# Second batch masked on VectorE, mask table built on chip, smaller value loads between the w_out pieces

## The chip, the core and the metric

The kernel runs on one core of one Trainium2 chip. The metric is the device time of one execution in microseconds; three executions of the kernel before gave 304.31, 306.18 and 306.58 us, so 306.18 us is its median. The profile is of one execution, which also took 306.18 us.

A core has engines with an instruction queue each, which works strictly in order: PE (TensorE, matmuls; PEld is its loading of weights), DVE (VectorE), ACT (ScalarE), POOL (GpSimd) and SP (SyncE, which here only starts DMA transfers). They wait for one another by semaphores.

## The reference

Windowed attention of 8 heads and then a two-layer network with a leaky ReLU, in float32:

```python
B, H, S, D = q.shape                     # 8, 8, 576, 64
scores = np.matmul(q, k.transpose(0, 1, 3, 2)) / np.sqrt(D)
rel = pos[:, None] - pos[None, :]
mask_plain = (rel >= 0) & (rel < 32)                       # heads 0 to 3
mask_dil = (rel >= 0) & (rel < 128) & (rel % 4 == 0)       # heads 4 to 7
attn = softmax(np.where(mask, scores, -1e9))
x = np.matmul(attn, v).transpose(0, 2, 1, 3).reshape(4608, 512)
h = x @ w_in                             # 512 x 2048
out = np.maximum(0.01 * h, h) @ w_out    # 2048 x 512
```

## The kernel before

**Attention.** A batch is worked as four pairs of heads (`vi` 2, 3, 0, 1: the dilated ones first), each as two units `u`. A unit (function `unit`) makes its scores with five matmuls (L724), takes their exponential on ACT (L731, tile `ee`), and multiplies them by the ones (L741 with `con`, the sums) and by the values (L741 with `slots`). ACT turns the sums into reciprocals by a logarithm and an exponential (L752, L754, tile `rc`), and DVE writes the normalised result into `xt` (L765). The scores have to be masked. For batches 0 and 1 (`by_pe`) PE adds a bias of 0 or -60000 to them ahead of the scores: two or three matmuls of the identity by columns of `con` (L720). For batches 2 to 7 DVE multiplies the exponentials by a table of zeros and ones in `con` (L735). The table, 1600 columns, is a repetition of three small patterns (a band of 96 columns and two of 32). It is loaded whole from memory, as the step `c` of the list `FIRST`.

**Loads of batches 0 and 1.** q and k are cast to 16 bits (tile `nat`, L369 and L371), turned by PE (L612; the 64 last rows at L653) and copied to `slots` by DVE and ACT (L382, L384). Values are cast from `vst` to `slots`. Later batches load q and k in narrow columns and turn them on DVE (L577 to L589).

**The network.** `up` (L784) multiplies `xt` by `w_in` in chunks of 384 tokens, or half chunks of 192 for chunk 1, and ACT applies the leaky ReLU into `gt` (L799). `down` (L823) multiplies the first four tiles of 128 tokens by `w_out`, each in four groups of four matmuls; group p needs the pieces 2p and 2p + 1 of `w_out`, which arrive as `w8` to `w15` and are cast by DVE and POOL. Later tiles go in fours through `group`, which needs seven block products in place of eight (L913, with sums and differences on DVE at L853, L899 and L950). `last_seven` does the same for three chunks of the first layer (L1099, L1124, L1173 to L1200).

**What sets the order.** No instruction stands where the code names it. Every operation is a task with an engine (or a choice of engines), a duration, and a latency until others see it. `_Plan` runs through these tasks in a forward and a backward pass, nine times, and the best order found is written out, engine by engine. `MARGIN`, from the time `CALM` on, scales the durations that the plan believes; `LATE` is added to the landing of a load. The loads of batches 0 and 1 and of the weights are fixed in the sequence of the string `FIRST` (q and k of half a batch `q01`, the last rows `r0`, values `v01`, weight pieces `w0` to `w15`, the table `c`) and go through SP, with eight transfers out at most. After the plan, `idle` (L1289) puts in filler matmuls where the plan leaves PE without work ahead of batch 0's first results.

**Around the change.** The constants' first part (identity, ones, biases; L402) is loaded by ACT's queue; the first memsets (L376) and eight warm-up matmuls (L1027) run meanwhile.

Of the kernel before, what the change touches and what calls it, by code (L numbers as in the profile page):

```python
# [12 lines left out]
ALU = mybir.AluOpType  # L13
# [14 lines left out]
FIRST = ('q01 r0 q00 w0 v01 v00 w1 w2 w3 w4 w5 w6 w7 q11 r1 q10 v11 w8 w9 w10 w11 v10 '  # L28
         'w12 w13 c w14 w15')


def _constants():

    ident = np.eye(128, dtype=np.float16)
    key = np.arange(128)[:, None] % 64
    rel = np.arange(96)[None, :] - key
    band = (rel >= 0) & (rel < WIN)
    last = []
    for half in range(2):
# [3 lines left out]
    plain0 = [band] * 4 + [band[:, :32]]  # L43
    plain1 = [band] * 3 + [band[:, :64], band[:, 32:]]
    dils = [[band, band, band[:, :80], band[:, :80], last[i]] for i in range(2)]
# [3 lines left out]
    return np.concatenate([x.astype(np.float16) for x in (ident, pairs, bias, table)], axis=1)  # L49


class _Task:
# [16 lines left out]
class _Plan:  # L69
# [179 lines left out]
def kernel(  # L249
# [14 lines left out]
    B, H, S, D = q.shape  # L264
# [6 lines left out]
    HS = S * D  # L271
    EARLY = 2
# [6 lines left out]
    def sbuf(name, shape, dt=FP16):  # L279
        return sb.tile(shape, dt, name=name)  # L280
# [13 lines left out]
    M_PAIR, M_BIAS, M_TAB = 128, 256, 256 + 160  # L294
    NCON = M_TAB + 1600
    con = sbuf("con", [128, 2112])
# [176 lines left out]
    def load_rest(b, prio, queue="SP"):  # L473
        _, r_old = ring("REST", 1, r_users := [])
        sn, s_old = ring("STG", NST, s_users := [])
        st, c = stg[sn], []
        for o, src in ((0, q), (1, k)):
            lo = load(queue, at(st, 0, 64, o * 512, [64, 8], [1, 64]),
                      dram(src, b * H * HS + 512 * D, [D, 64], [HS, 8], [1, D]),
                      512, 256, s_old, prio + 0.1 * o)  # L480
            c += [cast(at(rest, 0, 64, o * 512 + 256 * g, [128, 2], [64, 2], [1, D]),
                       at(st, 0, 64, o * 512 + 256 * g, [64, 2], [128, 2], [1, D]), 256, [lo] + r_old, prio)
                  for g in (1, 0)]
        s_users += c
        raw[b, "rest"] = c, r_users

    def load_v(b, g, prio, queue="SP"):
        base = (b * H + 4 * g) * HS
        vn, v_old = ring("VST", NVS, v_users := [])
        vs = vst[vn]  # L490
        lv = []
        if g == 0:
            for hh in range(2):
                p0 = 64 * hh
                lo = load("SP", at(vs, p0, p0 + 64, 0, [D, 18], [1, D]),
                          dram(v, base + 2 * hh * HS, [D, 64], [64 * D, 18], [1, D]),
                          1152, 256, v_old, prio + 0.01 * hh)
                lv.append([[lo], [lo]])
        else:
            for hh in range(2):  # L500
                p0 = 64 * hh
                c_in = load(queue, at(vs, p0, p0 + 64, 512, [S, 2], [1, D]),
                            dram(v, base + 2 * hh * HS + 512 * D, [D, 64], [HS, 2], [1, D]),
                            128, 256, v_old, prio + 0.02 + 0.01 * hh)
                ab = [load("SP", at(vs, p0, p0 + 64, j * S, [256, 2], [1, 256]),
                           dram(v, base + (2 * hh + j) * HS, [4 * D, 64], [256 * D, 2], [1, 256]),
                           128, 1024, v_old, prio + 0.01 * hh + 0.005 * j) for j in range(2)]
# [20 lines left out]
    def load_w(n, prio):  # L528

        home, off, prev = w_home[n]  # L530
        f = home if home.dtype == FP32 else home.bitcast(FP32)
        st = f[:, off:off + 1024]
        users = w_used[n]
        old = w_used[prev] if prev is not None else []
        if n < 8:
            vi = ORDER[n % 4]
            x = n // 4 * 1024
            src = dram(moe_w_in, heads_of(vi)[0] * D * DFF + x, [DFF, 64], [2 * D * DFF, 2], [1, 1024])
            dst, x = w_in, vi * DFF + x
        else:  # L540
            x = 1024 * (n - 8)
            src = dram(moe_w_out, 128 * x, [2 * DM, 128], [1, 1024])
            dst = w_out
        t = load("SP", st, src, 128, 4096, old, prio, 1.0, 1.0)
        for i in range(2):
            c = cast(dst[:, x + 512 * i:x + 512 * i + 512], st[:, 512 * i:512 * i + 512], 512, [t],
                     prio, ("POOL", "DVE"))
            users.append(c)
            if n < 8:
                for j in range(n // 4 * 8 + 4 * i, n // 4 * 8 + 4 * i + 4):  # L550
                    w_in_t[j, vi] = c
            else:
                w_out_t[2 * (n - 8) + i] = [c]
# [123 lines left out]
    def unit(b, vi, u, prio, banks):  # L677
        dil = vi >= 2
        tn = slot_of[b, vi]
        users, old = slot_users[b, vi]  # L680
        by_pe = b < EARLY
        p_bank, v_bank = (banks[(bank_at[0] + i) % len(banks)] for i in range(2))
        bank_at[0] += 2
        p_old, p_users = grab(p_bank)
# [31 lines left out]
        def scores(e):  # L716
# [6 lines left out]
            for i, (s, qd, qx, c, w, _, _) in enumerate(steps):  # L723
# [7 lines left out]
                  lambda e: nc.scalar.activation(out=et[:, 0:n], in_=p_bank[:, 0:n], func=AF.Exp,  # L731
                                                 scale=SCALE), prio)
        t_m = t_e if by_pe else add(
            "DVE", 0.45, 0.15, [t_e, t_con[0]],
            lambda e: nc.vector.tensor_tensor(out=et[:, 0:n], in0=et[:, 0:n],  # L735
                                              in1=con[:, table:table + n], op=ALU.mult), prio)

        def second(dst, lhs):
            def fn(e):
# [290 lines left out]

    clock = [-1500.0]

    def tick():
        clock[0] += 1
        return clock[0]

    t_con = [None]
    for b in range(EARLY):
        take_slots(b)
    for step in FIRST.split():  # L1040
        kind = step[0]
        if kind == "w":
            load_w(int(step[1:]), tick())
        elif kind == "c":
            t_con[0] = load("SP", con[:, M_TAB:NCON], const_d[:, M_TAB:NCON], 128, 3200, [], tick())
        else:
            b = int(step[1])
            if kind == "q":
                load_qk(b, int(step[2]), tick())
            elif kind == "v":  # L1050
                load_v(b, int(step[2]), tick())
            else:
                load_rest(b, tick())

    def attend(b, first, step):
        if b >= EARLY:
# [283 lines left out]
```

## Time and profile before

| what | value |
|---|---|
| the profiled execution | 306.18 us |
| its span, first to last instruction | 303.1 us |
| PE busy | 287.6 us (95%) |
| DVE, ACT, POOL busy | 218.1, 218.6, 135.2 us |
| mean granted PE clock | 0.994 |
| moved by DMA | 47.15 MB, 156 GB/s over the span |
| constants: first part / table | 104 KB / 400 KB |

In the profile a line such as `L784 PE MATMUL hps<-xt,w_in` gives the line of the kernel, the engine, the operation, and the tiles written and read. A timeline row has the start and the length in us, and in square brackets how long its engine had been idle before it and whom it had waited for. A row of the view by stretches has, for each engine, its busy time and in brackets its instructions, then the granted PE clock, the share of the DMA engines' time and the GB/s. In the chain of waits each row has a start, a length and what the end of the kernel hung on in that time.

### The profile page before, as it was taken

Reading aid. Unit: us, or ns where it says so; the run is one execution under the profiler, and the core shown is the slowest. Engines: PE = TensorE matmul, PEld = TensorE weight load, DVE = VectorE, ACT = ScalarE, POOL = GpSimd, SP = SyncE. Lnnn points to the kernel's source line nnn. Section 1 sums busy time; section 2 is a strip of 40 time slices with the busy share of each in tenths; the row PEclk is TensorE's granted clock in tenths of the full one; section 3 lists DMA queues with packets and bytes.
Section 4 is the critical chain, followed back from the end, with each engine's and each line's share of the span. In section 5 each row is a group of like instructions: output and inputs, shape, how many; then the busy total and the mean of one; then the engine's idle time right before and its main releaser. Section 6 shows DMA issues by size and latency. Waiting matters only on the chain.

```text
span 303.1 us, 7895 instructions
## 1 busy us (share of the span) xinstructions
PE 287.6 (95%) x3035; PEld 228.5 (75%) x3035; DVE 218.1 (72%) x389; ACT 218.6 (72%) x509; POOL 135.2 (45%) x191
## 2 busy tenths in 40 slices
PE   5689879999999999999999999999799999999995
PEld 2575567568777789777777877767588999999984
DVE  6685575677569978936867768889985886568842
ACT  2787787558897766788888867978576788868411
POOL 5265523584759855782982953778500000000000
PEclk9889999999999999999999999999999999999999
DMA  7999899889989959998997299691010210030122
GB/s 228 319 397 348 257 238 353 128 170 199 159 176 208 193 135 169 214 205 140 212 184 145 50 186 189 139 229 46 29 44 35 71 37 1 2 107 35 37 104 104
DMA packets 156068, 47.15 MB, mean 156 GB/s; under 512 B 136832, under 2 KB 153344, under 8 KB 156032
## 3 DMA queue, kind: packets, MB, share of 16 engines
q1 hardware_dynamic: 155344, 46.04, 64.4%
q10 hardware_dynamic: 688, 0.63, 0.7%
q8 instruction: 23, 0.38, 0.5%
q14 instruction: 13, 0.11, 0.1%
HBM read 37.22 MB, written 9.44 MB: 154 GB/s over the span
## 4 chain that ended last, share of the span: by engine, by line
PE 77%; DMA 9%; DVE 6%; ACT 2%; SPq 2%; POOL 1%; issue 1%; DVEq 0%; POOLq 0%; ACTq 0%
PE hps L784 23%; PE fps L913 20%; PE tp L913 8%; PE hps L1173 4%; PE ops L1173 4%; PE ops L741 4%; DMA xt<-in_moe_w_out_dram 3%; PE fps L823 3%; DMA stg<-in_k_dram 3%; DMA gt<-in_moe_w_out_dram 2%; PE sps L741 2%; SPq L357 2%; PE ops L724 2%; PE sps L1173 1%; PE hps L1027 1%
## 5 line engine op out<-in xcount | busy, mean ns | idle before, releaser
L784 PE MATMUL hps<-xt,w_in 128*128 128x384 f16 (+1 forms) x616 | 109.4, 309 | 0.7 <-DVE xt L765 0.3
L799 ACT ACTIVATE gt<-hps 128x384 f16<-128x384 f32 (+1 forms) x154 | 69.5, 458 | 20.6 <-PE hps L784 19.2
L913 PEld LDWEIGHTS <-gt 128*128 128x128 f16 x768 | 72.8, 98 | 10.6
L784 PEld LDWEIGHTS <-w_in 128*128 128x128 f16 x640 | 55.5, 98 | 24.0 <-issue 1.2
L371 POOL CAST slots<-vst 64x576 f16<-64x576 f32 x54 | 49.6, 936 | 8.6 <-DMA vst<-in_v_dram 7.0
L913 PE MATMUL fps<-w_out,gt 128*128 128x256 f16 x368 | 47.3, 272 | 0.0
L371 POOL CAST nat<-stg 128x576 f16<-128x576 f32 (+1 forms) x52 | 38.2, 756 | 14.1 <-DMA stg<-in_k_dram 8.2
L735 DVE TENSOR_TENSOR ee<-ee,con 128x384 f16<-128x384 f16 (+1 forms) x48 | 26.3, 549 | 19.3 <-ACT ee L731 19.1
L384 POOL COPY slots<-turned 64x64 f16<-64x64 f16 (+2 forms) x41 | 22.5, 556 | 28.2 <-DVE turned L577 27.2
L754 ACT ACTIVATE rc<-rc 128x288 f32<-128x288 f32 x64 | 28.1, 445 | 1.1
L765 DVE TENSOR_TENSOR xt<-ops,rc 128x288 f16<-128x288 f32 x42 | 18.9, 449 | 11.8 <-ACT rc L754 5.0
L741 PEld LDWEIGHTS <-con 128*128 128x128 f16 x320 | 20.0, 99 | 8.4 <-issue 4.5
L724 PEld LDWEIGHTS <-slots 128*128 128x128 f16 x320 | 19.0, 99 | 5.2 <-issue 1.3
L731 ACT ACTIVATE ee<-ops 128x384 f16<-128x384 f32 (+1 forms) x41 | 20.5, 502 | 3.4 <-PE ops L724 3.2
L752 ACT ACTIVATE rc<-ops 128x288 f32<-128x288 f32 x41 | 16.8, 410 | 6.2 <-PE ops L741 5.8
L942 ACT COPY stg<-fps 128x512 f32<-128x512 f32 (+1 forms) x24 | 12.8, 532 | 10.6 <-PE fps L913 10.1
L741 PEld LDWEIGHTS <-slots 128*128 128x128 f16 x320 | 17.9, 97 | 3.2 <-ACT slots L369 0.3
L1200 ACT ACTIVATE gt<-slots 128x384 f16<-128x384 f32 x36 | 17.9, 527 | 1.9 <-DVE slots L1193 1.7
L577 DVE STREAM_TRANSPOSE turned<-nat 128x576 f16<-128x576 f16 x24 | 18.0, 762 | 0.8 <-POOL nat L371 0.8
L382 ACT COPY slots<-turned 64x512 f16<-64x512 f16 (+1 forms) x25 | 16.6, 664 | 1.2 <-DVE turned L577 0.7
L899 DVE TENSOR_TENSOR gt<-gt 128x1024 f16<-128x1024 f16 x21 | 17.0, 813 | 0.1
L823 PE MATMUL fps<-w_out,gt 128*128 128x512 f16 x64 | 16.2, 378 | 0.3 <-DVE w_out L371 0.2
(121 smaller groups left out, 501.0 us busy)
## 6 DMA issues: line engine op xcount, KB each, us to landing
out_dram<-osb SPq DMA_DIRECT2D x32, 256.0 KB, 2.8
stg<-in_q_dram SPq DMA_DIRECT2D x48, 144.0 KB, 3.4
stg<-in_k_dram SPq DMA_DIRECT2D x48, 144.0 KB, 3.6
vst<-in_v_dram SPq DMA_DIRECT2D x16, 288.0 KB, 4.6
vst<-in_v_dram SPq DMA_DIRECT2D x32, 128.0 KB, 3.1
gt<-in_moe_w_in_dram SPq DMA_DIRECT2D x6, 512.0 KB, 6.7
stg<-in_q_dram SPq DMA_DIRECT2D x3, 512.0 KB, 7.1
stg<-in_k_dram SPq DMA_DIRECT2D x3, 512.0 KB, 7.6
```

Of the source, the lines that this page charges most:

```text
L371: ENG[e].tensor_copy(out=dst, in_=src)
L384: ENG[e].tensor_copy(out=dst, in_=src)
L724: nc.tensor.matmul(p_bank[:, c:c + w], slot(tn, KB + 128 * s, 0, 128, [1, 128]), slot(tn, qx, 0, 128, *qd), start=first or not by_pe, stop ...
L731: lambda e: nc.scalar.activation(out=et[:, 0:n], in_=p_bank[:, 0:n], func=AF.Exp, scale=SCALE), prio)
L735: lambda e: nc.vector.tensor_tensor(out=et[:, 0:n], in0=et[:, 0:n], in1=con[:, table:table + n], op=ALU.mult), prio)
L741: nc.tensor.matmul(at(dst, 0, 128, o, *od), lhs(s), et[:, c:c + w], start=i == 0, stop=i == len(steps) - 1, skip_group_check=True)
L754: lambda e: nc.scalar.activation(out=rt, in_=rt, func=AF.Exp, scale=-1.0), prio)
L784: nc.tensor.matmul(ht[:, 0:n], at(w_in, 0, 128, vi * DFF + j // 2 * 256 + j % 2, [2, 128]), at(xt[m % 2], 0, 128, vi * 1152 + x0 + x, [1, n]),
L799: lambda e: nc.scalar.activation(out=gt[c % NG][:, j * n_c + x:j * n_c + x + n], in_=ht[:, 0:n], func=AF.Prelu, alpha=0.01),
L823: nc.tensor.matmul(ft, g[:, j * n_c + tt * 128:j * n_c + tt * 128 + 128], w_out[:, j * DM:j * DM + DM], start=(j == 0), stop=(j == NJ - 1))
L913: nc.tensor.matmul(bk[:, x:x + HN], tl[:, off + j * step:off + j * step + 128], rhs(j), start=first and x == 0 and j == 0, stop=j == HJ - ...
L1173: nc.tensor.matmul(b[:, i * HT:i * HT + HT], lhs(v, j0 + i), rhs(v), start=first and i == 0 and v == 0, stop=i == 1 and v == 1, skip_group ...
```

## The change

Five things are done at once.

- `by_pe` holds for batch 0 only. Batch 1's eight units are masked at L735 by DVE like those of later batches.
- The table is no longer loaded. The first load of constants takes the three patterns along (576 columns in place of 416), and eight copies on DVE or POOL, as the plan chooses, repeat them into the table. A multiply waits for the copies of its part of the table.
- `load_v` can place each of its transfers in the sequence on its own. A dot in `FIRST` is the place of the next such transfer. Batch 1's values of the plain heads (`v10`) come in four transfers of 64x9x64 in place of two of 64x18x64.
- `FIRST` is another sequence: `w8` stands ahead of batch 1's first q and k, `w9` between its halves, and the small value loads stand between the pieces of `w_out`.
- The plan's constants differ: `LATE` is 1.5 and not 0.5, a load of the list is counted as later the further down it stands (`RAMP`), and `MARGIN` and `CALM` have other values. So the whole order is planned anew on every engine.

```diff
-ROOM, LATE = 256, 0.5
+ROOM, LATE = 256, 1.5
+RAMP = 1.93
-MARGIN = {'ACT': 1.037, 'DVE': 1.092, 'POOL': 1.059, 'PE': 0.981, 'SP': 1.0, 'DMA': 1.155, 'LAND': 1.118}
-CALM = 45.0
+MARGIN = {'ACT': 1.045, 'DVE': 1.084, 'POOL': 1.042, 'PE': 1.0, 'SP': 1.0, 'DMA': 1.23, 'LAND': 1.076}
+CALM = 33.2
-FIRST = ('q01 r0 q00 w0 v01 v00 w1 w2 w3 w4 w5 w6 w7 q11 r1 q10 v11 w8 w9 w10 w11 v10 '
-         'w12 w13 c w14 w15')
+FIRST = ('q01 r0 q00 w0 v01 . . . . . v00 . w1 w2 w3 w4 w5 w6 w7 w8 q11 r1 v11 . w9 . '
+         'q10 . . . w10 w11 v10 w12 . w13 . . w14 w15')
...
-    bias = np.where(np.concatenate([band] + last, axis=1), 0.0, -60000.0)
-    table = np.concatenate(plain0 + plain1 + dils[0] + dils[1], axis=1)
+    mask = np.concatenate([band] + last, axis=1)
+    bias = np.where(mask, 0.0, -60000.0)
...
-                     (0.5 if prio < -1400 else LATE) if late is None else late)
+                     ((0.5 if prio < -1400 else LATE) if late is None else late)
+                     + (RAMP * max(0.0, prio + 1500) / 40 if prio < -1400 else 0.0))
...
-    def load_v(b, g, prio, queue="SP"):
+    def load_v(b, g, prio, at_step=None):
...
+        def when(x):
+            n[0] += 1
+            return at_step[n[0] - 1] if at_step else prio + x
+        for hh in range(2):
+            p0 = 64 * hh
+            if g == 0 and b == 1:
+                lv.append([[load("SP", at(vs, p0, p0 + 64, j * S, [D, 9], [1, D]),
+                                 dram(v, base + (2 * hh + j) * HS, [D, 64], [64 * D, 9], [1, D]),
+                                 576, 256, v_old, when(0.01 * hh + 0.005 * j))] for j in range(2)])
...
-        by_pe = b < EARLY
+        by_pe = b == 0
...
         t_m = t_e if by_pe else add(
-            "DVE", 0.45, 0.15, [t_e, t_con[0]],
+            "DVE", 0.45, 0.15, [t_e] + t_con[u if not dil else 2],
             lambda e: nc.vector.tensor_tensor(out=et[:, 0:n], in0=et[:, 0:n],
-                                              in1=con[:, table:table + n], op=ALU.mult), prio)
+                                              in1=con[:, table:table + n], op=ALU.mult), prio,
+            0.0, "m")
...
+    def table_part(dst, dims, src, from_dims, n):
+        def fn(e):
+            ENG[e].tensor_copy(out=at(con, 0, 128, M_TAB + dst, *dims),
+                               in_=at(con, 0, 128, M_BAND + src, *from_dims))
+        return add((("DVE", 0.11 + n * 0.0006), ("POOL", 0.07 + n * 0.0011)), None, 0.2, [t_id], fn, 10.0)
+
+    t_con = [
+        [table_part(0, [[96, 4], [1, 96]], 0, [[0, 4], [1, 96]], 384),
+         table_part(384, [[1, 32]], 0, [[1, 32]], 32)],
+        [table_part(416, [[96, 3], [1, 96]], 0, [[0, 3], [1, 96]], 288),
+         table_part(704, [[1, 64]], 0, [[1, 64]], 64),
+         table_part(768, [[1, 64]], 32, [[1, 64]], 64)],
+        [table_part(832, [[384, 2], [96, 2], [1, 96]], 0, [[0, 2], [0, 2], [1, 96]], 384),
+         table_part(832 + 192, [[384, 2], [80, 2], [1, 80]], 0, [[0, 2], [0, 2], [1, 80]], 320),
+         table_part(832 + 352, [[384, 2], [1, 32]], 96, [[32, 2], [1, 32]], 64)]]
...
-        elif kind == "c":
-            t_con[0] = load("SP", con[:, M_TAB:NCON], const_d[:, M_TAB:NCON], 128, 3200, [], tick())
```

More of the change, by code (lines that the diff above doesn't have):

```diff
@@ L42, in _constants @@
         last.append((key % 4 == res) & (key // 4 <= u))
-    plain0 = [band] * 4 + [band[:, :32]]
-    plain1 = [band] * 3 + [band[:, :64], band[:, 32:]]
-    dils = [[band, band, band[:, :80], band[:, :80], last[i]] for i in range(2)]
-    bias = np.where(np.concatenate([band] + last, axis=1), 0.0, -60000.0)
-    table = np.concatenate(plain0 + plain1 + dils[0] + dils[1], axis=1)
+    mask = np.concatenate([band] + last, axis=1)
+    bias = np.where(mask, 0.0, -60000.0)
     pairs = np.arange(128)[:, None] // 64 == np.arange(128)[None, :] % 2
-    return np.concatenate([x.astype(np.float16) for x in (ident, pairs, bias, table)], axis=1)
+    return np.concatenate([x.astype(np.float16) for x in (ident, pairs, bias, mask)], axis=1)
 class _Task:
@@ L490, in load_v @@
         vs = vst[vn]
[L491 to L494, printed above, removed]
+        lv, n = [], [0]
+        def when(x):
[7 more added lines that the diff above has]
+                                 576, 256, v_old, when(0.01 * hh + 0.005 * j))] for j in range(2)])
+            elif g == 0:
                 lo = load("SP", at(vs, p0, p0 + 64, 0, [D, 18], [1, D]),
                           dram(v, base + 2 * hh * HS, [D, 64], [64 * D, 18], [1, D]),
-                          1152, 256, v_old, prio + 0.01 * hh)
+                          1152, 256, v_old, when(0.01 * hh))
                 lv.append([[lo], [lo]])
[L499 to L504, printed above, removed]
+            else:
                 ab = [load("SP", at(vs, p0, p0 + 64, j * S, [256, 2], [1, 256]),
                            dram(v, base + (2 * hh + j) * HS, [4 * D, 64], [256 * D, 2], [1, 256]),
-                           128, 1024, v_old, prio + 0.01 * hh + 0.005 * j) for j in range(2)]
+                           128, 1024, v_old, when(0.01 * hh + 0.005 * j)) for j in range(2)]
+                c_in = load("SP", at(vs, p0, p0 + 64, 512, [S, 2], [1, D]),
+                            dram(v, base + 2 * hh * HS + 512 * D, [D, 64], [HS, 2], [1, D]),
+                            128, 256, v_old, when(0.02 + 0.01 * hh))
                 lv.append([[ab[j], c_in] for j in range(2)])
@@ L1031 @@
     clock = [-1500.0]
[L1033 to L1037, printed above, removed]
+    def table_part(dst, dims, src, from_dims, n):
[12 more added lines that the diff above has]
+         table_part(832 + 352, [[384, 2], [1, 32]], 96, [[32, 2], [1, 32]], 64)]]
     for b in range(EARLY):
         take_slots(b)
-    for step in FIRST.split():
-        kind = step[0]
-        if kind == "w":
-            load_w(int(step[1:]), tick())
-        elif kind == "c":
-            t_con[0] = load("SP", con[:, M_TAB:NCON], const_d[:, M_TAB:NCON], 128, 3200, [], tick())
[L1046 to L1053, printed above, removed]
+    steps = FIRST.split()
+    rows, waiting = {}, []
+    for i, step in enumerate(steps):
+        if step[0] == "v":
+            rows[step] = [clock[0] + 1 + i]
+            waiting += [step] * {"v01": 5, "v11": 5, "v00": 1, "v10": 3}[step]
+        elif step == ".":
+            rows[waiting.pop(0)].append(clock[0] + 1 + i)
+    assert not waiting
+    for i, step in enumerate(steps):
+        kind, prio = step[0], clock[0] + 1 + i
+        if kind == "w":
+            load_w(int(step[1:]), prio)
+        elif kind == "q":
+            load_qk(int(step[1]), int(step[2]), prio)
+        elif kind == "v":
+            load_v(int(step[1]), int(step[2]), prio, rows[step])
+        elif kind == "r":
+            load_rest(int(step[1]), prio)
     def attend(b, first, step):
```

5 lines of the change are left out of this document (2 added, 3 removed).

## The prediction

> **What bounds the kernel now.** I read the page's engine rows and slices first, then the chain that ended last, then the PE's order of time between 30 and 62 us, and last its waits.
>
> ```profile
> PE 287.6 (95%) x3035; PEld 228.5 (75%) x3035; DVE 218.1 (72%) x389; ACT 218.6 (72%) x509; POOL 135.2 (45%) x191
> PE   5689879999999999999999999999799999999995
> DMA  7999899889989959998997299691010210030122
> ```
>
> PE is busy for 287.6 of 303.1 us. In stretches, its idle time is 9.7 us before 60 us (3.05 of it the wait for the first memset) and 5.8 us after, of which some 3.5 is the tail of the last evictions and stores. The page's DMA row is near full for the first seven slices, so the start is shared by PE and the loads. The chain of waits says how:
>
> ```profile
> 26.72 7.59 DMA stg<-in_k_dram
> ...
> 34.78 6.95 DMA gt<-in_moe_w_out_dram
> ...
> 46.00 9.54 DMA xt<-in_moe_w_out_dram
> ...
> 55.59 0.88 POOL w_out L371
> ```
>
> From 26.7 to 55.6 us the chain runs over loads, and it ends in the last w_out piece. From there it is PE almost alone. The same moment on PE (start, length, matmuls, idle before):
>
> ```profile
> 53.69 0.34 PE L720 MATMUL ops<-con 128*128 128x384 f16 x2
> 53.88 0.35 PE L724 MATMUL ops<-slots 128*128 128x96 f16 x5
> ...
> 55.27 0.59 PE L823 MATMUL fps<-w_out,gt 128*128 128x512 f16 x2
> 56.04 0.85 PE L823 MATMUL fps<-w_out,gt 128*128 128x512 f16 x2 [0.18 <-DVE w_out L371]
> ```
>
> PE waits only 0.18 us for that piece: it gets there as the piece does. **Two limits therefore meet near 55.5 us**, PE's own work and the last load, and time falls only by the smaller of what the two give up. Afterwards the work is fixed and PE is 237.3 us busy of 243.1; its waits there add up to 2.2 us (total, times, longest):
>
> ```profile
> PE ops L741 <- DVE ee L735: 1.1, 2, 0.7
> PE sps L741 <- DVE ee L735: 0.9, 1, 0.9
> PE ops L724 <- DVE xt L765: 0.2, 1, 0.2
> ```
>
> **Part 1, the bias matmuls of batch 1 go.** Batch 1 has 8 units. In each, L720's group stands ahead of the scores; from its first start to L724's (36.94 to 37.12, 38.09 to 38.27, and so on to 56.73 to 56.91) it takes 0.17 to 0.19 us. Eight sum to 1.45 us of PE, 1.27 of it ahead of the 55.27 us matmuls and 0.18 behind. The changed order has 22 matmuls fewer at this line. It has three more 128x256 fillers (L1289), all before batch 0's work is done; one costs 0.11 us at the spacing of the 128x512 rows (9.01 us, 0.82 for three with the drain), so 0.33 us, in places where the order expects a wait. I take 0; bounds 0 to +0.33.
>
> **Part 2, the masks on DVE.** Eight multiplies come in at L735.
>
> ```profile
> L735 DVE TENSOR_TENSOR ee<-ee,con x48: 310/376/1533, 68.2 to 234.0; 128x384 f16<-128x384 f16 x24, 128x416 f16<-128x416 f16 x24
> ```
>
> At the mean of 549 ns that is 4.4 us of DVE, between 2.5 (min) and 12.3 (max). DVE is busy 10.2 of 18 us between 38 and 56 us, so there is room. What matters is the hand-over: from the scores (72.08) over the exponential to the end of the multiply (73.33) is 1.25 us with a 0.36 us multiply. I counted, at the spacing of the rows, the matmuls that the changed order puts between a unit's scores and its first L741: 2.3, 2.6, 1.6, 2.1, 2.1, 1.4, 2.1 and 2.3 us. All are above 1.25, the tightest by 0.2. Behind a late L741, PE's in-order queue stands still. I take 0; the bounds are nothing and rival B.
>
> [...] At 213.46, 215.53 and 198.22 us one took 0.92, 0.92 and 1.53 us while POOL was casting; at 220.43 and 221.90, with POOL done, 0.35. [...] POOL is busy 5.6 of those 18 us against 45% over the span, so I stay with the mean.
>
> **Part 3, the table.** The 400 KB load goes, and 40 KB join the first one. In its place stand eight copies: five on DVE (1,088 elements a partition), three on POOL (512), all right behind the first memsets and ahead of the first casts. No row shows a 16-bit copy within SBUF. The nearest are the cast at 4.42 us (0.36 for 512) and the copy from PSUM (0.43): 0.77 to 2.2 us on DVE. The cover: PE's warm-up matmuls last until 6.65 us and its first transposes follow at once, while the casts they need end by 6.0; the last cast waits for a load until 6.64 anyway. The cover of some 0.6 us is gone if the copies take above 1.2 us. I take 0; bounds 0 to +0.9. POOL's next cast waits for a load until 7.13, so its copies are free.
>
> **Part 4, the last w_out piece lands earlier.** The order of loads up to it is otherwise the same 7.5 MB, so it comes earlier by 400 KB at the rate of that stretch:
>
> ```profile
> 32.00:38.00 6.00, 4.89 (x50) 3.35 (x49) 3.95 (x10) 3.99 (x10) 2.54 (x4) 1.00 0.86 239
> 48.00:52.00 4.00, 4.00 (x49) 3.05 (x48) 1.89 (x4) 2.60 (x9) 1.89 (x3) 1.00 1.02 407
> ```
>
> At 407 GB/s it is 1.0 us, at 239 it is 1.7. SP needed 4.84 us (28.18 to 33.02) to issue batch 1's six small v loads, 576 KB, and the queue then ran at 0.86 of its time; spread between 512 KB pieces they starve it less, worth 0 to 0.8 us (0.14 x 6). Against it stand 0.1 for the 40 KB. The four smaller v loads replace two of the same packets (169 GB/s at 42 to 46 us): two more issues of 0.6 us, under cover of a queue with work. I take 1.0 + 0.4 - 0.1 = 1.3; bounds 0.9 to 2.4.
>
> **Part 5, the order.** w_out pieces 0 and 1 now load ahead of batch 1's q and k, whose last piece comes 1.3 MB (some 4 us) later. In return the first two L823 groups move ahead of, and right behind, batch 1's first scores; before, PE lost 2.5 us between 33 and 44 us, mostly to slot copies. When the order reaches the group that needs the last piece, the same work is done in both kernels (16 half blocks of L784, six L823 groups, 7 units' scores, 6 sums), less 1.27 us of bias matmuls. PE can thus be there 1.27 us or more earlier, and the piece 1.3.
>
> **Sum.** -1.3 at the last piece, -0.18 for the eighth bias group, 0 behind it: -1.5 us. The profiled execution took 306.18 us (span 303.1 and 3.1 around it), which is also the median. **Forecast 304.7 us.**
>
> **Rivals.**
> A, the later waits vanish as well: all new constants re-plan what follows 60 us, and the 2.2 us above may go. 304.7 - 2.2 = 302.5. For it: these waits come from multiplies queued behind long DVE work, which the new order places anew. Against it: nothing in the change aims there, and the list may as well make new ones.
>
> B, slower: PE stands on the masks of batch 1. With multiplies of 0.92 us (213.46) each behind a cast and a slot copy (0.43 and 0.69 at 42.96 and 43.40), the hand-over is 1.25 + 0.56 + 1.12 = 2.9 us. Over the eight gaps PE waits 0.6 + 0.3 + 1.3 + 0.8 + 0.8 + 1.5 + 0.8 + 0.6 = 6.7 us: 311.4. It starts to cost at a lateness of 0.2 us and eats up the gain at about 0.9 us for each multiply (0.7 + 0.1 + 0.1 + 0.7 + 0.1 = 1.7). For it: casts of w_out do stand between the multiplies in the changed DVE order. Against it: POOL's small share there.
>
> C, the change doesn't do what it says: the last piece is not earlier, because issue and landing wait for others (54 to 56 us show DMA at 0.10 of its time while that piece is out). PE then waits for it and keeps only 0.18: 306.0.
>
> D, the clock. Between 13.6 and 17.0 us the granted clock was 0.50, and five-matmul groups stood 0.32 us apart against 0.19 later; a second such stretch costs half of 3.4 us, 1.7: 306.4. [...]
>
> **How the numbers follow.** A measurement of this kernel (304.31 to 306.58) tells some 1%, 3.06 us, from no change. Chances: forecast 0.45, A 0.20, B 0.15, C 0.12, D 0.08. Only A is faster by over 1%: 0.20. B is slower by over 1%: 0.15. The rest, 0.65, is within. The forecast's own bounds (gain 2.4 + 0.2; loss 0.9 + 0.3 of start, partly absorbed) give 303.6 to 306. The range takes in A, C and D and the lower part of B: 302.0 to 308.0.
>
> **What would show it.** Right: the last w_out landing near 54.2 us, its L823 group near 54.2 with a short wait, L720 with 22 matmuls, no PE wait above 0.3 us on L735 before 60. Wrong: sums of batch 1 waiting on L735 (B), a landing still near 55.5 (C), a second 0.50 clock (D), or other waits after 60 us than 1 to 3 us (A, or its mirror, which would give 306.9).

## The result

The changed kernel is slower: 308.61 us at the median (307.53 to 311.26) against 304.34 us of the kernel before beside it, a ratio of 1.0123 with a 95% interval of 1.0086 to 1.0161. The forecast was 304.7 us with a range of 302.0 to 308.0. It was worked out as 1.5 us less than the 306.18 us of the profiled execution; beside the median of 304.34 us the number 304.7 is no gain, so the forecast to hold against the runs is the difference of -1.5 us.

The profiled execution took 311.26 us, the longest of its seven, with a span of 309.4 us. Its page, the rows that answer to those of before, and the row of the main DMA queue (packets, which are the pieces that loads and stores are moved in, MB, and the time that the packets took as a share of 16 engines' span):

```profile
PE 286.3 (93%) x3016; PEld 226.4 (73%) x3016; DVE 221.7 (72%) x400; ACT 222.3 (72%) x513; POOL 136.3 (44%) x192
...
PE   5868776799999999999999999999899999999995
...
DMA  8999999789998997997997189898001210031133
...
q1 hardware_dynamic: 155232, 45.63, 67.6%
```

PE has 1.3 us less to do than before (287.6), as forecast, and the span is 6.3 us longer in this pair of profiles (the medians are 4.3 us apart). But for the last slice, the digits below 8 in PE's row are all in the first eight slices. The last row looks harmless, but before, the same queue moved 0.41 MB more in 64.4% of a shorter span:

```profile
q1 hardware_dynamic: 155344, 46.04, 64.4%
```

The chain of waits of the changed kernel between 15 and 62 us (start, length, what the end hung on):

```profile
17.64 6.41 DMA gt<-in_moe_w_in_dram
24.04 11.91 DMA stg<-in_q_dram
...
37.23 8.94 DMA vst<-in_v_dram
...
46.18 11.21 DMA vst<-in_v_dram
...
59.97 0.83 DVE w_out L369
...
61.09 0.35 DVE w_out L369
```

The chain is one load after another, and the last piece of `w_out` is cast from 61.0 us on, one half by POOL and one by DVE (61.09). Before it was at 55.6, and the forecast had it near 54.2. Why the loads are late is seen in the view by stretches (PE, PEld, DVE, ACT and POOL busy, granted clock, DMA share, GB/s). First the changed kernel, then the kernel before:

```profile
6.00:8.00 2.00, 1.29 (x15) 0.88 (x14) 1.33 (x5) 0.78 (x2) 0.28 (x1) 1.00 1.25 204
14.00:18.00 4.00, 2.83 (x37) 1.74 (x35) 2.78 (x6) 3.47 (x8) 1.93 (x2) 1.00 1.34 197
0.00:60.00 60.00, 43.99 (x472) 29.84 (x473) 34.59 (x82) 38.78 (x94) 27.62 (x45) 1.00 1.06 265
60.00:310.00 250.00, 242.27 (x2544) 196.58 (x2543) 187.12 (x320) 183.49 (x420) 108.67 (x148) 1.00 0.60 123
```

```profile
6.00:8.00 2.00, 1.92 (x16) 1.19 (x15) 1.16 (x5) 0.64 (x2) 0.64 (x2) 1.00 1.16 322
14.00:18.00 4.00, 3.50 (x47) 3.02 (x45) 3.48 (x7) 3.78 (x9) 3.61 (x5) 0.62 1.13 330
0.00:60.00 60.00, 50.33 (x545) 34.96 (x546) 38.86 (x83) 40.10 (x99) 26.20 (x44) 0.97 0.97 285
60.00:310.00 250.00, 237.31 (x2491) 193.56 (x2489) 179.24 (x307) 178.51 (x411) 109.01 (x148) 0.99 0.56 120
```

Between 6 and 8 us and between 14 and 18 us the DMA engines are busier than before (1.25 against 1.16, 1.34 against 1.13 of their time) and move some 40% less. They do not starve; **packets take longer**. Between 6 and 8 us, with the same first loads under way in both kernels, packets of 1024 bytes take 95 ns at the median in place of 46. Between 14 and 18 us a part of the difference is another mix: the kernel before already moves weights there, in packets of 4096 bytes (three quarters of its bytes), and the changed one still mostly packets of 256. PE gets 6.3 us less done by 60 us. It has 5.0 us more to do afterwards (242.3 in place of 237.3). The span grew by 6.3 us with 1.3 us less work, so PE idles 7.6 us more: 6.3 ahead of 60 us and 1.3 after it.

### The profile page after: what moved, and what is told of

It is laid out like the page before. It is cut to its first block, busy times and chain, and to the rows that moved or that the text cites. A ratio compares the mean times of both kernels' runs of the same rounds, so it can differ in the third digit from the quotient of the medians.

```text
span 309.4 us, 7881 instructions
## 1 busy us (share of the span) xinstructions
PE 286.3 (93%) x3016; PEld 226.4 (73%) x3016; DVE 221.7 (72%) x400; ACT 222.3 (72%) x513; POOL 136.3 (44%) x192
## 3 DMA queue, kind: packets, MB, share of 16 engines
q1 hardware_dynamic: 155232, 45.63, 67.6%
## 4 chain that ended last, share of the span: by engine, by line
PE 65%; DMA 20%; DVE 5%; SPq 4%; POOL 2%; issue 2%; ACT 1%; POOLq 0%; DVEq 0%; ACTq 0%
PE hps L789 20%; PE fps L918 18%; DMA vst<-in_v_dram 10%; PE tp L918 8%; DMA stg<-in_q_dram 5%; PE hps L1193 4%; PE ops L1193 4%; SPq L354 4%; PE ops L746 3%; PE fps L828 2%; DMA stg<-in_k_dram 2%; DMA gt<-in_moe_w_in_dram 2%; PE sps L746 2%; PE ops L728 2%; PE sps L1193 1%
## 5 line engine op out<-in xcount | busy, mean ns | idle before, releaser
L789 PE MATMUL hps<-xt,w_in 128*128 128x384 f16 (+1 forms) x616 | 108.1, 309 | 4.4 <-ACT gt L804 3.6
L804 ACT ACTIVATE gt<-hps 128x384 f16<-128x384 f32 (+1 forms) x154 | 68.8, 456 | 20.4 <-PE hps L789 18.1
L789 PEld LDWEIGHTS <-w_in 128*128 128x128 f16 x640 | 56.3, 98 | 29.2 <-issue 5.2
L369 POOL CAST slots<-vst 64x576 f16<-64x576 f32 x53 | 48.2, 926 | 12.2 <-DMA vst<-in_v_dram 10.7
L369 POOL CAST nat<-stg 128x576 f16<-128x576 f32 (+1 forms) x54 | 40.4, 772 | 15.5 <-DMA stg<-in_k_dram 7.3
L739 DVE TENSOR_TENSOR ee<-ee,con 128x384 f16<-128x384 f16 (+1 forms) x56 | 30.3, 545 | 14.1 <-ACT ee L735 14.0
L382 POOL COPY slots<-turned 64x64 f16<-64x64 f16 (+2 forms) x38 | 20.4, 542 | 26.2 <-DVE turned L581 14.5
L770 DVE TENSOR_TENSOR xt<-ops,rc 128x288 f16<-128x288 f32 x42 | 18.9, 450 | 11.2 <-ACT rc L759 10.4
L728 PEld LDWEIGHTS <-slots 128*128 128x128 f16 x320 | 18.9, 97 | 6.7 <-issue 1.8
L735 ACT ACTIVATE ee<-ops 128x384 f16<-128x384 f32 (+1 forms) x41 | 20.5, 503 | 3.7 <-PE ops L728 3.5
L746 PEld LDWEIGHTS <-slots 128*128 128x128 f16 x320 | 17.3, 97 | 5.3 <-POOL slots L369 1.7
L380 ACT COPY slots<-turned 64x512 f16<-64x512 f16 (+1 forms) x27 | 17.9, 662 | 1.6 <-DVE turned L581 1.1
L587 POOL COPY slots<-turned 128x576 f16<-128x576 f16 x12 | 9.3, 774 | 17.9 <-DVE turned L586 10.7
L746 PE MATMUL ops<-ee,slots 128*128 128x96 f16 (+3 forms) x210 | 14.2, 199 | 2.8 <-POOL slots L369 1.5
```

The lines of the kernel that those rows point to most:

```text
L369: ENG[e].tensor_copy(out=dst, in_=src)
L382: ENG[e].tensor_copy(out=dst, in_=src)
L728: nc.tensor.matmul(p_bank[:, c:c + w], slot(tn, KB + 128 * s, 0, 128, [1, 128]), slot(tn, qx, 0, 128, *qd), start=first or not by_pe, stop ...
L746: nc.tensor.matmul(at(dst, 0, 128, o, *od), lhs(s), et[:, c:c + w], start=i == 0, stop=i == len(steps) - 1, skip_group_check=True)
L770: lambda e: nc.vector.tensor_tensor(out=at(xm, 0, 128, x, *dst), in0=at(v_bank, 0, 128, 0, *src), in1=at(rt, 0, 128, 0, *src), op=ALU.mult ...
L789: nc.tensor.matmul(ht[:, 0:n], at(w_in, 0, 128, vi * DFF + j // 2 * 256 + j % 2, [2, 128]), at(xt[m % 2], 0, 128, vi * 1152 + x0 + x, [1, n]),
```

## Experiments, first round: undoing parts

The first suspects were the named parts of the change. Each of four runs undoes one of them in the changed kernel. All were taken beside the kernel before at 304.73 us.

**The list undone** (run e1): before's sequence but for the table, with `v10` in two transfers.

```diff
-FIRST = ('q01 r0 q00 w0 v01 . . . . . v00 . w1 w2 w3 w4 w5 w6 w7 w8 q11 r1 v11 . w9 . '
-         'q10 . . . w10 w11 v10 w12 . w13 . . w14 w15')
+FIRST = ('q01 r0 q00 w0 v01 v00 w1 w2 w3 w4 w5 w6 w7 q11 r1 q10 v11 w8 w9 w10 w11 v10 '
+         'w12 w13 w14 w15')
```

> The changed kernel with the old sequence of early loads (table still left out, batch 1's plain values in two transfers, no load ahead of its half batch); masks, table copies and plan constants stay as changed. Theory L (the list): small value loads of 64 partitions between the w_out pieces slow each other's packets, the 4096-byte packets from 0.16 to some 0.23 us between 40 and 56 us, and put the last w_out piece and batch 1's values late; so without it the last piece lands near 54 to 56 us and the time is 303 to 305 us. Rival P (the plan's constants) expects 307 to 309, rival M (masks) 307 to 309.

Measured: 310.10 us, ratio 1.0164 (1.0106 to 1.0223). The list is not the cause.

**The planner's numbers undone** (run e2).

```diff
-ROOM, LATE = 256, 1.5
-RAMP = 1.93
+ROOM, LATE = 256, 0.5
+RAMP = 0.0
```

with `MARGIN` and `CALM` as before's too.

> The changed kernel with the old LATE 0.5, no RAMP, old MARGIN and CALM; list, masks and table copies as changed. Theory L: the loads still come late, 307 to 310 us, last w_out piece near 60 us. Rival P (the plan, counting loads later, puts instructions late or in a worse order in the in-order queues): 303 to 305 us.

Measured: 311.23 us, 1.0209 (1.0155 to 1.0264). Nor are the numbers.

**The masks undone** (run e3).

```diff
-        by_pe = b == 0
+        by_pe = b < EARLY
```

> The changed kernel with batch 1 masked by PE's bias matmuls again. Theory L: 308 to 310 us, since 1.45 us of PE comes back while PE waits for loads anyway. Rival M (PE stands on the masks of batch 1): 304 to 306 us.

Measured: 309.88 us, 1.0154 (1.0085 to 1.0223). Nor the masks.

**The table loaded again** (run e4), ahead of `w14`, in place of the eight copies.

```diff
-         'q10 . . . w10 w11 v10 w12 . w13 . . w14 w15')
+         'q10 . . . w10 w11 v10 w12 . w13 . . c w14 w15')
```

> The changed kernel with the 400 KB table loaded again ahead of w14 and no copies on chip. Theory L: 308 to 311 us, 1 us of loads more ahead of the last piece. A rival that the copies at the start delay the first casts and all that follows: 306 to 307 us, first w_in issue near 12 us as before the change and not near 13.5.

Measured: 315.84 us, 1.0355 (1.0306 to 1.0403), the slowest of the four. A second loss comes in here; it is taken up below.

No part undone brought the time back. That leaves a combination of parts, or something that the changed kernel and all four share. One line of the diff, which neither the description of the change nor the prediction had spoken of, is in all of them:

```diff
-    con = sbuf("con", [128, 2112])
+    con = sbuf("con", [128, M_TAB + 1600])
```

The tile `con` grows from 2112 to 2176 columns of 16 bits, by 128 bytes in each partition. Tiles are placed one behind another, `con` first, so everything behind it moves by 128 bytes: `stg0`, where queries and keys land, goes from byte 53504 of a partition, a multiple of 256, to byte 53632, 128 past one. The same holds for `vst`, `xt`, `gt` and `wst`, where values and weights land.

## Experiments, second round: the addresses alone

**The changed kernel with con of 2368 columns** (run g1): tiles back on their multiples of 256, nothing else touched; every instruction and its order on every engine is the same, and the combination of parts stays.

```diff
-    con = sbuf("con", [128, M_TAB + 1600])
+    con = sbuf("con", [128, 2368])
```

> The changed kernel with one number altered: the tile con has 2368 columns of fp16 in place of 2176 (4736 bytes of a partition in place of 4352), 512 bytes more than before's 4224, so that every tile behind it lies where before has it, plus 512 bytes. Every instruction and its order on every engine is unchanged. Address theory (A): the four undone parts left the early packets slow (in the trace of the changed kernel 256-byte packets take 26 to 29 ns at the median between 12 and 18 us, before 18 to 21), and the one thing that all of them shared with the changed kernel was con's size, which moves every later tile by 128 bytes; so here the time falls by 4 to 6 us to 302 to 305 us, the last w_out cast ends near 54 us in place of 61, and the 256-byte packets are back at 18 to 21 ns. Rival R (the new order of instructions itself costs the time, whichever part is undone): 308 to 310 us, the last w_out cast at 60 to 62 us.

Measured: 305.62 us against 305.68, ratio 0.9996 (0.9949 to 1.0043). The loss is gone, though the time lies 0.6 us above the 302 to 305 us that were expected. The queue's row, and the view by stretches of this kernel:

```profile
q1 hardware_dynamic: 155232, 45.63, 64.5%
```

```profile
14.00:18.00 4.00, 3.00 (x41) 2.11 (x41) 3.89 (x9) 3.93 (x10) 1.83 (x3) 1.00 1.15 317
0.00:60.00 60.00, 47.87 (x512) 32.36 (x513) 39.16 (x90) 41.62 (x101) 28.21 (x48) 1.00 1.00 277
```

The same packets as in the changed kernel take 64.5% in place of 67.6%, the stretch of 14 to 18 us is back at 317 GB/s from 197, and PE does 3.9 of the missing 6.3 us by 60 us. Another 1.3 us of the 6.3 is bias work that is no longer there; the rest, some 1.2 us, the changed order does not win back.

**The kernel before with con of 2176 columns** (run g2): the same step, alone, the other way.

```diff
-    con = sbuf("con", [128, 2112])
+    con = sbuf("con", [128, 2176])
```

> The kernel before with one number altered: the tile con has 2176 columns in place of 2112, as the changed kernel has it. Every instruction and its order is before's own. Theory A (addresses): 4 to 6 us slower than before, 308 to 311 us, 256-byte packets at 26 ns or more between 12 and 18 us, the last w_out piece cast 3 us or more after before's 55.6. Rival R (order): 304 to 305 us, no difference.

Measured: 308.65 us, 1.0117 (1.0047 to 1.0188): the loss of the whole change, from a number that alters no instruction. Its queue and its stretch of 14 to 18 us:

```profile
q1 hardware_dynamic: 155344, 46.04, 67.6%
```

```profile
14.00:18.00 4.00, 3.71 (x43) 3.21 (x42) 2.70 (x6) 3.51 (x9) 1.22 (x2) 0.57 1.23 196
```

330 GB/s have become 196 (in g2 none of the weights' large packets has come by then). PE's waits after 60 us are those of before to a tenth, so the loss lies ahead of them. The engines' own instructions are hardly slower at the new addresses: PE, DVE and ACT are busy 288.6, 218.8 and 218.4 us, in the kernel before 287.6, 218.1 and 218.6. In the DMA issues (KB each, median us from issue to landing) the 512 KB loads of queries and keys show it; first the kernel before, then g2:

```profile
stg<-in_q_dram SPq DMA_DIRECT2D x3, 512.0 KB, 7.1
stg<-in_k_dram SPq DMA_DIRECT2D x3, 512.0 KB, 7.6
```

```profile
stg<-in_q_dram SPq DMA_DIRECT2D x3, 512.0 KB, 9.8
stg<-in_k_dram SPq DMA_DIRECT2D x3, 512.0 KB, 10.7
```

**Which tile?** Two runs take g1 and put 128 bytes of padding ahead of one group of tiles, and 128 behind it: the value tiles (run j3) or the five staging tiles (run j4).

```diff
+    pad0 = sbuf("pad0", [128, 64])
     vst = [sbuf(f"vst{i}", [128, 1152], FP32) for i in range(NVS)]
+    pad1 = sbuf("pad1", [128, 64])
```

> The changed kernel with con of 2368 columns (all tiles on 256-byte multiples) and 128 bytes of padding ahead of the two vst tiles and 128 behind them, so that only the landing place of the value loads is off. Order unchanged. Theory V (the small value loads, 64 partitions each, are where the packets get slow, so their landing place decides): 307.5 to 309 us as the changed kernel, 256-byte packets at 25 ns or more between 12 and 18 us. Rival Q (all loads pay alike): about a third of the loss, 306 to 307 us. Rival N (weights and queries decide): 305 to 306 us.

> The changed kernel with con of 2368 columns and 128 bytes of padding ahead of the five stg tiles and 128 behind them: only the landing place of queries and keys (and of what else is staged there) is off. Order unchanged. Theory V: 305 to 306 us, as all aligned; 256-byte packets between 12 and 18 us at 18 to 22 ns, 1024-byte packets of 128 partitions at 51 ns. Rival Q: 306 to 307 us. Rival N: 307 to 309 us.

Measured: 306.15 us for the values, ratio to before 1.0035 (0.9997 to 1.0073), and 307.23 us for the staging tiles, 1.0060 (1.0018 to 1.0102). Theory V, that the small value loads alone decide, falls. The staging tiles pay a part, clear of nothing; for the value tiles the interval just reaches 1, and only their slower packets (in the table below) speak for a part, as rival Q has it. The difference between the two is within their intervals.

**How far off?** Three runs take the kernel before with other widths of `con`, so that the tiles start 32, 64 or 224 bytes past a multiple of 256.

```diff
-    con = sbuf("con", [128, 2112])
+    con = sbuf("con", [128, 2128])     # 32 past;  64: 2144;  224: 2224
```

> The kernel before with con of 2128 columns in place of 2112: every tile behind it starts 32 bytes past a multiple of 256 in its partition (before: on a multiple; the changed kernel: 128 past one). Order unchanged. Theory A1 (any start off a 256-byte multiple costs, because a packet then touches one block of 256 bytes more): slower than before, 306.5 to 309 us, ratio 1.005 to 1.012; 256-byte packets between 12 and 18 us at 22 ns or more at the median, 1024-byte packets alone at 47 to 51 ns. A2 (only the size of the piece in the first block counts: 32 bytes cost little): 305 to 306.5 us, packets at before's 18 and 46 ns. [...]

> The kernel before with con of 2224 columns: every tile behind it starts 224 bytes past a multiple of 256. Order unchanged. A1 (one block more, wherever the start): as the 32-byte kernel beside it and as con of 2176, 307 to 309.5 us. A2 (the bytes on the far side count): as con of 2176 or worse where the bytes ahead of the start are moved too (308 to 312 us), or like the 32-byte kernel where only the smaller piece counts. [...] Rival S (the 512-byte grid matters): not told apart here, 308 us or more.

> The kernel before with con of 2144 columns: every tile behind it starts 64 bytes past a multiple of 256. Order unchanged. Starts 128 past cost 3 to 4 us (308.7), starts 32 and 224 past cost 8 to 9 us (313.9, 312.8), and with those two the share of packet time on the main queue is 79% in place of 67.6% and 64.4%. Theory G (two grids: a packet that crosses one more 256-byte line costs a little, and a packet whose ends are off a 64-byte grid costs more): as 128 past, 307.5 to 309.5 us, share 66 to 69%. Rival E (128 is the one half that is cheap): as 32 and 224, 312 to 315 us, share 76 to 80%.

Measured: 313.94 us for 32 (1.0307; 1.0224 to 1.0390), 312.03 for 64 (1.0223; 1.0170 to 1.0277), 312.77 for 224 (1.0246; 1.0175 to 1.0317). None of the expectations written first had these sizes: the three are alike, as A1 has it, but they cost 7 to 9 us and not the 1.5 to 4. Theory G, with a second grid of 64 bytes, falls with 64, and rival E, that 128 is the one cheap start, has the time right. The queue's rows, for 32 and then for 64 bytes:

```profile
q1 hardware_dynamic: 155344, 46.04, 79.1%
```

```profile
q1 hardware_dynamic: 155344, 46.04, 81.0%
```

The packet records of the traces say why 128 is the cheaper half. Mean time of one packet on the main queue, in ns, by its size, and the sum over all packets divided by 16 engines:

| tiles start past a multiple of 256 by | run | 128 B | 256 B | 1024 B | sum, us |
|---|---|---|---|---|---|
| 0 | before | 12.9 | 19.0 | 50.7 | 195.1 |
| 0 | g1 | 12.9 | 18.9 | 50.9 | 196.5 |
| 128 | after | 13.1 | 22.9 | 54.7 | 209.2 |
| 128 | g2 | 13.0 | 22.7 | 56.7 | 208.3 |
| 64 | p1 | 18.2 | 26.3 | 57.2 | 250.7 |
| 32 | j2 | 17.4 | 26.6 | 57.7 | 246.2 |
| 224 | j5 | 17.3 | 26.5 | 59.5 | 246.9 |
| 128, `vst` alone | j3 | 13.1 | 22.2 | 52.2 | 204.5 |
| 128, `stg` alone | j4 | 12.9 | 19.6 | 52.0 | 197.9 |

110,592 packets have 128 bytes: the columns of later batches' queries and keys. Laid down 128 past a multiple, each still lies within one block of 256 bytes and takes 13 ns as before. Laid down 32, 64 or 224 past, in a row of such packets every second one lies, by its address, across a block's edge. Their median stays at 13 ns, but about a third of them take 16 ns or more, against 1 in 100 in the kernel before. That adds 30 to 37 us of packet time on each of the 16 engines between 56 and 214 us, beside the loss at the start. How it reaches PE is not the same in each: after 60 us PE waits 4.9 us for masks in j2 and 2.1 in p1, against 2.0 before and in g2. Packets of 256 and 1024 bytes cross, by their addresses, one edge more from any start that is off, and are longer in all five kernels that are off throughout (22.7 to 26.6 ns against 18.9 and 19.0, and 54.7 to 59.5 against 50.7 and 50.9). One grid of 256 bytes, an inference from these rows, so gives the direction of every row. It doesn't by itself say why packets of 256 bytes are milder at 128 (23 ns) than at the other starts (26), with one edge each. Ahead of 56 us, where hardly any packets of 128 bytes run, they are nearly alike: 28 and 29 ns at 128, 29 to 30 at 32, 64 and 224, and 21 in place. Between 60 and 150 us they differ, 20 against 24 to 26; there they share the queue with the lengthened packets of 128 bytes, and that this is the reason was not tried.

The profile of j4 in the table is of one of its fastest executions, 305.69 us, so its row may show less than the median run has.

## Experiments, third round: the rest of the change with the tiles in place

With `con` at a multiple that keeps the tiles in place, single parts were put on before's list and numbers; the copies are those of the changed kernel.

**Masks on DVE and table copied on chip, together** (h2, then again with more repetitions, and with 2240 columns, where the staging tiles stand on multiples of 512).

```diff
-        by_pe = b < EARLY
+        by_pe = b == 0
...
-         'w12 w13 c w14 w15')
+         'w12 w13 w14 w15')
```

> Two of the change's parts on before's own list and planner numbers: batch 1 masked by VectorE and the table copied together on chip; list, split of v10 and the planner's numbers are before's, and con has 2368 columns so that the tiles lie as before's do modulo 512 bytes. Theory A: 302.5 to 305 us (parts 1 to 4 of the prediction, worth up to 1.5 us, without the list). Rival R: 308 us or more, since the order is planned anew here too.

> Masks of batch 1 on VectorE and table copied on chip, with before's list, split and planner numbers, as in the run with con of 2368 columns, now 2240 columns: the staging tiles start on multiples of 512 bytes. Theory A (256-byte multiples are what counts): as that run, 302.5 to 304.7 us, ratio 0.992 to 0.998, the share of packet time on the main queue near 64%. Rival S (512-byte multiples count): below 302 us, the share of packet time clearly lower.

> Masks and table on before's list and planner numbers, con of 2368 columns, once more with five rounds, since the run with 2240 columns came out between it and before (0.9978 against 0.9957). Theory A with parts 1 to 4 of the prediction: 303.5 to 305 us, ratio 0.994 to 0.998 with an interval below 1. Rival C (nothing gained): ratio 0.998 to 1.002.

Measured: 304.18 us, 0.9957 (0.9914 to 0.9999); with 2240 columns 304.91, 0.9978 (0.9944 to 1.0013); again 305.17, 1.0017 (0.9985 to 1.0050). The first looked like the forecast gain; repeated with more executions it is not there, and the last interval leaves out 0.995, which -1.5 us would be. Multiples of 512 give nothing over 256 (rival S falls). No version was found that beats the kernel before.

**The table alone** (h3: copied on chip, all early masks on PE).

> One part alone on before's list and planner numbers: the table is copied together on chip (no load of 400 KB), masks of both batches stay on TensorE, con of 2368 columns. Part 4 of the prediction: the last w_out cast begins 1.3 us (0.9 to 2.4) ahead of before's 55.6 us and the time falls by up to that: 303.5 to 305 us. Rival A of the prediction (later waits vanish too): 302.5 us. Rival C (nothing gained): 305 to 306 us.

Measured: 304.63 us, 0.9988 (0.9942 to 1.0033): within the range of part 4, and not told from nothing.

**The masks alone** (n2: batch 1 on DVE, the table still loaded ahead of `w14`).

> One part alone: batch 1 masked by VectorE, table still loaded before w14, list and planner numbers as before's, con of 2368 columns. Parts 1 and 2 of the prediction: TensorE's busy time falls by 1.4 to 1.5 us from 287.6, the masks cost nothing, the time falls by 0 to 1.5 us: 303.5 to 305.5 us. Rival B of the prediction (TensorE stands on the masks, or they wait for the table that lands late): 306 us or more, with waits of TensorE on the masks ahead of 60 us.

Measured: 316.24 us, 1.0345 (1.0277 to 1.0413). The masks stand in the way here, as in rival B, dearer than it was priced and for another reason: not the hand-over, but the table. Two rows of this kernel, for the multiplies and for the issue of the table's load (min/median/max ns, first and last start):

```profile
L737 DVE TENSOR_TENSOR ee<-ee,con x16: 323/413/1567, 53.9 to 95.8; 128x384 f16<-128x384 f16 x8, 128x416 f16<-128x416 f16 x8
...
L358 SPq DMA_DIRECT2D con<-consts x1: 423/423/423, 47.2 to 47.2; - x1
```

The same multiplies in h2, where the copies made the table by 6 us:

```profile
L733 DVE TENSOR_TENSOR ee<-ee,con x18: 342/374/1509, 37.7 to 97.0; 128x384 f16<-128x384 f16 x10, 128x416 f16<-128x416 f16 x8
```

The load is issued at 47.2 us, and the first mask of batch 1 starts at 53.9 in place of 37.7. PE's busy time by 60 us is 45.5 us here and 51.1 in h2. Run e4, with the first mask at 57.6 us and 315.84 us, is the same case. Rival D comes on top in both: in n2 PE is busy for 1.7 of the 4 us from 68 us, and from 73 us the granted clock is 0.50 for 6.8 us; in e4 for 1.6 of the 4 us from 54 us, and from 59 us it is 0.50 for 6.8 us; that the idle time brings the low clock was not tried. So with the table's load at this place in the list the masks can't go to DVE, and the copies let them; an earlier load was not tried.

**The new list alone** (h5) and **the planner's new numbers alone** (h4).

> One of the change's parts on before: the new list with its small value loads between weight pieces and with v10 in more pieces; masks by TensorE for both batches, table loaded before w14, planner's numbers as before's, con of 2368 columns. Theory A: within 2 us of before, 303 to 307 us. Rival R: 308 us or more.

> One part alone: the planner's new numbers (LATE, RAMP, MARGIN, CALM) on before's list, with masks of both batches on TensorE and the table loaded, con of 2368 columns. Part 5 of the prediction (order: no cost, no gain): 304 to 306 us, ratio 0.996 to 1.004. Rival: the new numbers give away what masks and table gain (they were worth 1.3 us together, and the whole change with the old addresses nothing): 306 to 307.5 us.

Measured: the list 305.28 us, 0.9998 (0.9960 to 1.0035); the numbers 308.69 us, 1.0098 (1.0053 to 1.0143). The numbers on before's list cost 3 us, more than either expectation. The casts of `w_out` there, and PE's longest wait after 60 us, in its timeline:

```profile
L373 DVE CAST w_out<-xt x3: 423/427/428, 42.3 to 58.4; 128x512 f16<-128x512 f32 x3
```

```profile
94.91 1.55 PE L787 MATMUL hps<-xt,w_in 128*128 128x384 f16 x5 [2.38 <-DVE xt L768]
```

The last piece is cast at 58.4 us, 2.8 later than before. The wait is for a write of `xt` that stands on DVE behind two sums of 1.08 and 1.25 us, and as it ends, at 95 us, the granted clock falls to 0.50 for 3.4 us. Eight of the ten executions have a mean clock below 1.00 and take 306.4 to 310.2 us; the two at 1.00 take 306.1 and 307.3. How the loss divides between these was not tried. In the whole change with the tiles in place (g1) the time is that of before, so with the new list the numbers do no such harm.

## Why the prediction was wrong

**The step that failed is part 4**: the last `w_out` piece "comes earlier by 400 KB at the rate of that stretch". It took before's rate as given. The rate fell, over the first 60 us from 285 to 265 GB/s (277 with the tiles in place, g1), mostly because the tiles had moved by 128 bytes, and the piece was cast 5.5 us later and not 1.3 earlier. In g2, with the order of before, the moved tiles alone make it 5.4 us later. The sum had no term for where tiles lie; the cause is a line of the diff that none of the five parts named. That this is the cause of the loss is shown from both sides, g1 and g2, with the same instructions in the same order. That g1's 305.62 us lies within the forecast's range is no merit of the sum: so does the kernel before.

Part 1 was right: TensorE has 1.3 us less to do (287.6 to 286.3; forecast 1.45, less up to 0.33 of fillers). The kernel before had 3.4 us at clock 0.50 in its profile; run e3 and the changed kernel, both at 1.00, have the same 287.6 and 286.3. But the gain counts only where the loads keep up, and they did not.

Part 2 was right under its condition: in g1, PE's waits on the masks of batch 1 by 60 us are 0.2 us in all, in the changed kernel 1.0.

```profile
PE ops L746 <- DVE ee L739: 0.2, 1, 0.2
```

Part 3 was right: the copies stand between 4.1 and 5.9 us. The five on DVE take 171 to 290 ns each, the three on POOL 423 to 592, and the view of PE's waits shows none on them:

```profile
L1040 DVE COPY con<-con x5: 171/198/290, 4.4 to 5.6; 128x320 f16<-128x320 f16 x1, 128x384 f16<-128x384 f16 x1, 128x32 f16<-128x32 f16 x1, 128x64 f16<-128x64 f16 x1
L1040 POOL COPY con<-con x3: 423/534/592, 4.1 to 5.1; 128x64 f16<-128x64 f16 x2, 128x384 f16<-128x384 f16 x1
```

Part 4's mechanism, with the tiles in place and before's list, came out: the last cast starts at 53.5 us in h3, at 52.8 and 54.8 in the two profiles of h2, and 54.3 with 2240 columns, 0.8 to 2.8 us earlier (forecast 1.3, bounds 0.9 to 2.4), though the two profiles of one kernel lie 2.0 us apart. With the new list this is not seen. In g1 the piece is there 0.7 us earlier, and DVE gets to its half only 1.8 us after POOL:

```profile
54.85 0.61 POOL L369 CAST w_out<-xt 128x512 f16<-128x512 f32 x1 [0.68 <-DMA xt<-in_moe_w_out_dram]
...
56.70 0.42 DVE L369 CAST w_out<-xt 128x512 f16<-128x512 f32 x1
```

In h5, which loads the table as before, it is cast at 56.9, 1.3 us later. Neither is more than those 2.0 us; the 0.4 us that part 4 had put down as a gain of the spread value loads no run shows.

Part 5 failed too, by less: PE was to be at the last piece 1.27 us earlier or more. In g1 it has done 47.9 us of work by 60 us, before 50.3; without the 1.3 us of bias work that is some 1.2 us behind. Its waits for ACT's writes of `gt` alone are 3.0 us there.

The sum of -1.5 us for what the parts do can't be told from zero: g1 gives 0.9996 (0.9949 to 1.0043), and masks with table 0.9957, 0.9978 and 1.0017. Of the rivals, C had the right symptom, a last piece that is not earlier, and not its size or cause. D did not come in the changed kernel, whose granted clock is 1.00 in its profile; it came in n2, e4 and h4. B came only where the table comes late, and not by its hand-over.

## What to carry to other kernels

A tile's size is part of every other tile's address. Before pricing a change, look for tiles that grow or shrink ahead of the landing places of loads, and keep those on multiples of 256 bytes (128 off cost 1.2% here, run g2); compare the queue's share of packet time and the GB/s of a stretch where DMA is the limit. Where undoing each named part leaves the loss in place, look for what all versions share.

## What was not expected of the hardware

A start 128 bytes off cost 1.2% of the run and one 32, 64 or 224 off 2.2 to 3.1%, with the same instructions in the same order: packets of 256 bytes went from 19 to 23 and 26 ns, and packets of 128 bytes from 13 to 17 or 18 ns only at 32, 64 and 224, where by their addresses every second one crosses a multiple of 256. These means hide how uneven it is. Between 12 and 18 us, where many small value loads are out, the median of packets of 256 bytes went from 18 to 22 ns up to 24 to 31 with the value tiles off. Between 60 and 150 us half of them still take 18 ns with tiles 128 off, as in place, and the mean is 20 in place of 18. So one edge more doesn't lengthen every packet; what else must come together was not tried.
